# Plain tiles in program order, with the attention stages placed by hand between half products

## The chip, the cores and the metric

The kernel runs on one core of a Trainium2 chip. The metric is the device time of one execution in microseconds (us); of several executions the median is given. In the rows PE is TensorE's matmul engine and PEld its weight loads, DVE is VectorE, ACT is ScalarE, POOL is GpSimd, and SP is SyncE, on whose queue all of this kernel's DMAs are issued. L650 means line 650 of the kernel before.

## What is computed

Three layers on 4608 tokens of width 512 (8 batches of 576 tokens, 8 heads of 64). Inputs of the last two layers' weights are float64, all else is float32.

```python
k_p = k.reshape(B, H, Sp, 8, D).mean(axis=3)          # keys and values pooled by 8: 72 of each
v_p = v.reshape(B, H, Sp, 8, D).mean(axis=3)
scores = np.matmul(q, k_p.transpose(0, 1, 3, 2)) / np.sqrt(D)
attn = softmax(scores)                                 # with 1e-9 added to the sum
x = tokens(np.matmul(attn, v_p))                       # (4608, 512)
h = x @ w_in                                           # 512 -> 2048
x = np.maximum(0.01 * h, h) @ w_out                    # 2048 -> 512
xn = x / sqrt(mean(x * x) + 1e-6) * rms_g
out = (silu(xn @ w_gate) * (xn @ w_val)) @ w_out2      # 512 -> 1536 -> 512
```

## The kernel before

Every float32 product is made of three matmuls of rounded parts (`TERMS`: high by high, high by low, low by high), so a value that TensorE multiplies lies in SBUF as a pair of tiles HI and LO; `split` makes such a pair with a ScalarE copy and a VectorE (or GpSimd) subtraction.

The 4608 tokens are nine tiles of 512. Tiles 0 to 6 are the plain tiles (`PLAIN` is 7): their first feed-forward layer is done as plain products. Tiles 7 and 8 do the same layer later, as a pair, by Strassen's products, and after them five pairs do the last layer in the same way. What those need of sums and parts of weights is made during the plain tiles by side steps (`side_steps`), on ScalarE, VectorE and GpSimd, and stored to DRAM.

A plain tile `j` runs over sixteen blocks `f` of 128 hidden units. `h_unit` makes `h` for one block: 12 matmuls into a bank of PSUM (tag `h`, two banks), 512 columns each. ScalarE then applies the ReLU twice, once into the HI tile and once into the float32 tile `g` in SBUF, and VectorE subtracts the one from the other for LO (lines 646 to 650). `y_unit`, for the block two before, adds 12 matmuls into four banks that hold the tile's output; `y_store` copies these out at the end. In tile 0 eight blocks are done in two parts, of 256 columns each.

The tokens come from attention, which runs beside the plain tiles, 40 steps of 128 queries (a batch has five). For one such step `step_t` transposes the queries, `step_s` makes the scores in two halves and the softmax, `step_x` transposes the result; for a part of a batch (`av0` 256 tokens, `av1` 320) `step_av` makes the output for four pairs of heads. `k_prep` and `v_prep` pool keys and values (on GpSimd from batch 1 on), `step_kt` transposes the keys. All transposes, the scores and the outputs go through two banks of PSUM (tag `att`). `top_up` issues the loads of queries, keys and values as their buffers come free.

Batch 0's steps come before tile 0 or in its first part (`before`, `second`). The steps of the others (`seq`) are divided by `SHARE` over places: even places are plain tiles, in which the steps are dealt over the slots between `h_unit` and `y_unit` (`attention_slot`), odd places are borders, whose steps are all run one after another at the end of a tile (`for x in border[j]`, lines 1450 and 1451). Tokens of a plain tile that lie more than about one tile ahead are split, stored to DRAM (`x_early`, line 394) and loaded again when their tile comes (`x_tile_loads`, line 407), because only two buffers (tag `xhl`) hold tokens. The order of all this on each engine is not the program's: a planner, which estimates the length of each instruction, chooses it up to the end of the plain tiles. From line 1466 on (`begun`) each engine's instructions are chained in program order (lines 1597 to 1604); that is the last two blocks of tile 6 and all that follows.

The parts of `w_out` for tiles 2 to 6: eight blocks rest in SBUF, eight pass through a ring of four buffers (`next_wo`, `RING` 4, line 725); the buffers that this frees hold the side steps' tiles. In the pairs, `Quad.result` (line 1259) does the same ReLU as `h_unit`, with the subtraction on GpSimd.

Of the kernel before, what the change touches and what calls it, by code (L numbers as in the profile page):

```python
# [17 lines left out]

TG = 3
# [5 lines left out]
def pooled_attention_then_two_ffns(  # L25
# [14 lines left out]
    B, H, S, D = q.shape  # L40
    NT, DM = out.shape
# [12 lines left out]
    PLAIN = NJ - 2  # L54
    QT = [0, 128, 256, 384, S - P]
    EAGER = 1
    H_STEPS, G_STEPS, P_STEPS, SIDE_END = 2, 5, 4, 128
    SHARE = (0, 0.13, 0.3, 0.475, 0.65, 0.825)
# [32 lines left out]
    eps = per.tile([P, 1], F32, name="eps")  # L91
    gain = per.tile([P, KC], F32, name="gain")
    ones = per.tile([P, P], F32R, name="ones")
# [106 lines left out]
    nc.gpsimd.memset(eps, 1e-6)  # L200

# [21 lines left out]
    def load_q(b, t, tile_=None):  # L223
        x = ap.tile([P, 512], F32, tag="q", bufs=2, name=f"q{b}_{t}") if tile_ is None else tile_
        nc.sync.dma_start(
            out=x.rearrange("p (h d) -> p h d", h=H),
            in_=q[b, :, QT[t]:QT[t] + P, :].rearrange("h s d -> s h d"),
        )
        qraw[b, t] = x
# [24 lines left out]
    def v_prep(b, r):  # L254
# [17 lines left out]
        )  # L272
        if rest:
# [45 lines left out]
    def step_s(b, t):  # L319
# [7 lines left out]
        for half in range(2):  # L327
            pt = bank("att", 2, f"sc{b}_{t}_{half}")
# [12 lines left out]
            )  # L341
        nc.scalar.activation(out=e, in_=e, func=AF.Exp, scale=ESCALE)
        nc.vector.tensor_reduce(out=st[:, 1, :], in_=e, axis=AX.X, op=ALU.add)
        nc.vector.tensor_scalar(out=st[:, 1, :], in0=st[:, 1, :], scalar1=1e-9, scalar2=None, op0=ALU.add)
# [8 lines left out]
    def step_x(b, t):  # L353
# [14 lines left out]
        for g in range(2):  # L368
            (nc.scalar.copy if b < 2 else nc.vector.tensor_copy)(
                out=er[:, g].rearrange("p d (q k) -> p d q k", q=2),  # L370
                in_=e[:, 2 * g:2 * g + 2, P:].unsqueeze(1).to_broadcast([P, 3, 2, REST]),
            )
        pt = scratch(b, f"xt{b}_{t}")
# [3 lines left out]
        split(nc.scalar, a[:, :, HI, cols], nc.vector, a[:, :, LO, cols], src)  # L377
        pt = scratch(b, f"xr{b}_{t}")
# [10 lines left out]
    place = [-1]  # L389
    x_dram = {j: dram.tile([P, KC, N], F32, name=f"x{j}") for j in range(PLAIN, NJ)}  # L390
    xh_dram = {}
    x_loads = {}

    def x_early(j, p, a, z, src):

        if j not in xh_dram:
            xh_dram[j] = dram.tile([P, 2, KC, N], F32, name=f"xh{j}")
        while a < z:
            e = min(z, a + N // 2)
            t = per.tile([P, 2, N // 2], F32R, tag="tg", bufs=TG, name=f"xs{j}_{p}_{a}")[:, :, :e - a]  # L400
            split(nc.scalar, t[:, HI], nc.vector, t[:, LO], src[:, :e - a])
            nc.sync.dma_start(out=xh_dram[j][:, :, p, a:e], in_=t.bitcast(F32))
            if p == NP - 1:
                x_loads.setdefault(j, []).append((a, e))
            src, a = src[:, e - a:], e

    def x_tile_loads(j):
        todo = sorted(x_loads.pop(j, ()))
        while todo:
            a, z = todo.pop(0)  # L410
            while todo and todo[0][0] == z:
                z = todo.pop(0)[1]
            for h in range(2):
                nc.sync.dma_start(out=x_tile(j)[:, h, :, a:z].bitcast(F32), in_=xh_dram[j][:, h, :, a:z])

    def x_tile(j):
        if j not in xhl:
            xhl[j] = per.tile([P, 2, KC, N], F32R, tag="xhl", bufs=2, name=f"xhl{j}")
        return xhl[j]

    def step_av(b, ci, p):
# [15 lines left out]
        while t0 < b * S + c1:  # L437
# [3 lines left out]
            if j >= PLAIN:  # L441
                x = per.tile([P, N], F32, tag="tg", bufs=TG, name=f"xs{b}_{ci}_{p}_{j}")[:, :t1 - t0]
                nc.scalar.copy(out=x, in_=pt[:, o:o + t1 - t0])
                nc.sync.dma_start(out=x_dram[j][:, p, t0 - j * N:t1 - j * N], in_=x)
                t0 = t1
                continue
            if place[0] < 2 * j - 3:
                x_early(j, p, t0 - j * N, t1 - j * N, pt[:, o:o + t1 - t0])
# [3 lines left out]
            split(  # L452
                nc.scalar, x[:, HI, p, t0 - j * N:t1 - j * N],
                nc.vector, x[:, LO, p, t0 - j * N:t1 - j * N], pt[:, o:o + t1 - t0],
            )
# [70 lines left out]
    END = 2 * PLAIN - 3  # L526
    low, high = [], []
    for kind, b, t in seq:
        lo, hi = 0, END
        if kind.startswith("av"):  # L530
            t0, t1 = (b * S + c for c in CH[int(kind[2])][:2])
            lo = 0 if t1 <= N * 2 else 2 * max(0, min((t1 - 1) // N, PLAIN - 1) - EAGER) - 3
            hi = min(2 * (t0 // N) - 1, END)
        low.append(max([lo] + low[-1:]))
        high.append(hi)
    for i in reversed(range(len(seq) - 1)):
        high[i] = min(high[i], high[i + 1])
    places, now = [[] for _ in range(2 * PLAIN)], 0
    for i, x in enumerate(seq):
        assert low[i] <= high[i]  # L540
        here = 2 * sum(i >= c * len(seq) for c in SHARE[1:])
        here = min(max(here, low[i], now), high[i])
        if here % 2 and here > max(low[i], now):
            here -= 1
        elif here % 2 and here < high[i] and not x[0].startswith("av"):
            here += 1
        places[here].append(x)
        now = here
# [1086 lines left out]
```

## Time and profile before

| | us |
|---|---|
| median of 3 runs (1880.48 to 1887.28) | 1884.13 |
| the profiled execution, its own time | 1889.12 |
| its span, first to last instruction | 1887.4 |
| lead: attention of batch 0, first weights | 0 to 40 |
| tile 0, to the last store of its output | 40 to 204 |
| tiles 1 to 5 | 204 to 812 |
| tile 6, no attention | 812 to 904 |
| the pair of tiles 7 and 8, then the last layer's pairs | 904 to 1887 |

The ends of the stages are the times at which the last DMA of a tile's output (line 689) was issued. TensorE is the busiest engine, with 94% of the span; VectorE has 50%, ScalarE 37%, GpSimd 33%. The chain of work that ended last has 81% of its time on TensorE. So time is lost where TensorE stands still, or where its clock is granted at the lower of its two levels, 1.2 instead of 2.4 GHz: a stretch whose mean is given as 0.61 had the lower level most of the time.

### The profile page before, as it was taken

The page shows a single profiled execution, that of the slowest core. Times are in us where ns is not written, and L with a number is a line of the kernel's source. Part 1 is how long each engine was busy: PE and PEld are TensorE (multiplying, and loading weights), DVE is VectorE, ACT ScalarE, POOL GpSimd, SP SyncE. Part 2 cuts the span into 40 slices and gives each one's busy share as a digit, 9 for nine tenths or more (in the row PEclk, how much of TensorE's full clock was granted, in tenths as well). Part 3 has the DMA queues.
Part 4 walks back from the last instruction along what each step waited for, and adds up shares of the span by engine and source line. Part 5 has one row for each costly group of instructions (what it writes and reads, how often), then busy time and mean ns, then how long its engine had stood idle before and what let it go on. Part 6 is the DMA issues. An engine that isn't in the chain of part 4 may idle for free.

```text
span 1887.4 us, 24256 instructions
## 1 busy us (share of the span) xinstructions
PE 1782.9 (94%) x8548; PEld 1511.7 (80%) x8548; DVE 938.9 (50%) x1691; ACT 697.9 (37%) x1476; POOL 630.6 (33%) x761
## 2 busy tenths in 40 slices
PE   3797999989898899899999999999999999999999
PEld 3787887878687787788778888899888889988887
DVE  8865435465555455452476544524734443563331
ACT  5653333333444344342455333224323323332220
POOL 2445215453432422020455344134224403422330
PEclk7898999999898999899999999999999999999999
DMA  8954204545565565274999765677775568776552
GB/s 263 391 193 145 77 20 142 173 130 196 156 204 161 170 203 174 78 244 126 337 316 310 233 211 186 230 277 250 268 241 194 200 228 293 252 265 205 201 201 89
DMA packets 215241, 388.54 MB, mean 206 GB/s; under 512 B 60752, under 2 KB 122192, under 8 KB 214352
## 3 DMA queue, kind: packets, MB, share of 16 engines
q1 hardware_dynamic: 215120, 386.99, 61.3%
q8 instruction: 68, 1.11, 0.2%
q14 instruction: 53, 0.43, 0.1%
HBM read 306.71 MB, written 80.22 MB: 205 GB/s over the span
## 4 chain that ended last, share of the span: by engine, by line
PE 81%; DMA 6%; DVE 5%; ACT 3%; POOL 2%; issue 2%; SPq 1%; ACTq 0%; POOLq 0%; DVEq 0%
PE o L1382 15%; PE h L637 13%; PE y L673 13%; PE yg L1253 6%; PE yv L1253 6%; PE o L1362 4%; PE xg L1253 4%; PE xv L1253 4%; PE wg L1253 4%; PE wv L1253 4%; PE yh L1253 2%; PE sc L331 2%; DMA y<-ye 2%; PE wh L1253 1%; PE xh L1253 1%
## 5 line engine op out<-in xcount | busy, mean ns | idle before, releaser
L637 PE MATMUL h<-xhl,w_i 128*128 128x512 f32 (+1 forms) x1440 | 350.0, 390 | 6.4 <-ACT g L104 3.9
L1382 PE MATMUL o<-wo,u 128*128 128x512 f32 x1296 | 316.3, 392 | 4.1 <-DMA wo<-wo 4.0
L637 PEld LDWEIGHTS h<-xhl,w_i 128*128 128x128 f32 x1440 | 265.0, 196 | 58.9 <-ACT g L104 7.1
L1382 PEld LDWEIGHTS o<-wo,u 128*128 128x128 f32 x1296 | 243.4, 189 | 53.5 <-DMA wo<-wo 4.9
L673 PE MATMUL y<-ghl,w_o 128*128 128x512 f32 (+1 forms) x1104 | 239.3, 360 | 3.2 <-ACT ye L686 1.4
L673 PEld LDWEIGHTS y<-ghl,w_o 128*128 128x128 f32 x1104 | 183.6, 191 | 31.1 <-ACT ghl L104 1.9
L650 DVE TENSOR_TENSOR ghl<-g,ghl 128x512 fp32r<-128x512 f32 (+1 forms) x120 | 90.5, 755 | 169.3 <-ACT g L104 164.2
L101 POOL TENSOR_TENSOR u<-e2g,u 128x512 fp32r<-128x512 f32 (+1 forms) x25 | 29.7, 1189 | 311.2 <-ACT u L98 311.2
L104 ACT ACTIVATE ghl<-h 128x512 fp32r<-128x512 f32 (+1 forms) x120 | 68.1, 567 | 163.6 <-PE h L637 162.4
L673 PE MATMUL y<-ghl,wr 128*128 128x512 f32 x432 | 111.6, 396 | 1.1 <-ACT ghl L104 1.1
L673 PEld LDWEIGHTS y<-ghl,wr 128*128 128x128 f32 x432 | 79.2, 188 | 17.2 <-ACT ghl L104 1.5
L235 POOL TENSOR_TENSOR v<-v 128x256 f32<-128x256 f32 (+3 forms) x84 | 55.0, 660 | 89.5 <-DMA v<-in_v_dram 85.0
L1253 PE MATMUL yg<-T,ag 128*128 128x512 f32 (+1 forms) x360 | 84.0, 368 | 0.0
L1253 PE MATMUL yv<-T,av 128*128 128x512 f32 (+1 forms) x360 | 83.8, 368 | 0.0
L1253 PE MATMUL xg<-xa,ag 128*128 128x512 f32 (+1 forms) x360 | 83.8, 367 | 0.0
L1253 PE MATMUL xv<-xa,av 128*128 128x512 f32 (+1 forms) x360 | 83.7, 367 | 0.0
L1253 PEld LDWEIGHTS yg<-T,ag 128*128 128x128 f32 x360 | 66.0, 188 | 10.0 <-DVE e1v L1230 0.6
L1253 PEld LDWEIGHTS yv<-T,av 128*128 128x128 f32 x360 | 66.2, 188 | 9.5
L1253 PEld LDWEIGHTS xv<-xa,av 128*128 128x128 f32 x360 | 66.0, 188 | 9.6
L1253 PEld LDWEIGHTS xg<-xa,ag 128*128 128x128 f32 x360 | 66.1, 188 | 9.4
L104 ACT ACTIVATE g<-h 128x512 f32<-128x512 f32 (+1 forms) x120 | 68.0, 567 | 12.9 <-DMA xh<-xs 6.2
L427 PE MATMUL av<-at,vb 128*128 128x256 f32 (+1 forms) x192 | 45.8, 357 | 20.0 <-DVE xs L101 6.9
(213 smaller groups left out, 3155.5 us busy)
## 6 DMA issues: line engine op xcount, KB each, us to landing
wo<-wo SPq DMA_DIRECT2D x148, 512.0 KB
ag<-op_g SPq DMA_DIRECT2D x90, 512.0 KB
av<-op_v SPq DMA_DIRECT2D x90, 512.0 KB
wr<-wo SPq DMA_DIRECT2D x36, 512.0 KB
op_g<-parts_g SPq DMA_DIRECT2D x36, 256.0 KB
op_v<-parts_v SPq DMA_DIRECT2D x36, 256.0 KB
out_dram<-oe SPq DMA_DIRECT2D x36, 256.0 KB
q<-in_q_dram SPq DMA_DIRECT2D x35, 256.0 KB
```

The costliest lines, as they stand in the source:

```text
L101: lo_eng.tensor_tensor(out=lo, in0=src, in1=hi.bitcast(F32), op=ALU.subtract)
L104: return nc.scalar.activation(out=out, in_=in_, func=AF.Prelu, scale=scale, alpha=alpha)
L235: nc.gpsimd.tensor_tensor(out=x[:, :n], in0=x[:, :n], in1=x[:, n:2 * n], op=ALU.add)
L331: nc.tensor.matmul(pt[:, i * n:(i + 1) * n], y[:, p, :], kblk[b % 2][:, p * n:(p + 1) * n], start=True, stop=True,)
L427: nc.tensor.matmul(pt[:, :n], vb[b, p][:, sp].rearrange("p h d -> p (h d)"), a[:, p, mp, 0:n], start=i == 0, stop=False,)
L637: nc.tensor.matmul(pt, w[:, sp, c * P:(c + 1) * P], x[:, mp, c, :], start=c == 0 and i == 0, stop=c == n_k - 1 and i == 2,)
L650: nc.vector.tensor_tensor(out=t[:, LO, :], in0=g, in1=t[:, HI, :].bitcast(F32), op=ALU.subtract)
L673: nc.tensor.matmul(pt, w[:, sp, m * P:(m + 1) * P], g[:, mp, a - c0:a - c0 + n], start=ydone[j, a] == 1 and i == 0 and m % per_bank == 0, ...
L1253: nc.tensor.matmul(pt, wt[:, a, c, sp, :], xt[:, mp, :], start=start and c == 0 and i == 0, stop=c == 1 and i == 2, skip_group_check=not s ...
L1362: nc.tensor.matmul(pt, w[:, sp, m * P:(m + 1) * P], u[:, mp, :], start=f == blocks(q, z)[0] and i == 0, stop=f == blocks(q, z)[-1] and i == 2,
L1382: nc.tensor.matmul(pt, u[:, sp, m * P:(m + 1) * P], w[:, mp, :], start=f == 0 and i == 0, stop=f == F2 - 1 and i == 2,)
```

## The change

Tile 0's first 14 of 24 units of work (`TIED`) stay as they were: the planner orders them, and the steps of batch 1 up to its first output (`mine`) are dealt over units 8 to 13. From there on `begun` is set, so each engine follows the program's order. There is no border, and nothing is dealt by shares: the program counts points, one after each half of an `h` product (6 matmuls of 512 columns) and one after each half of a `y` product, 28 in the rest of tile 0, 64 in each of tiles 1 to 5 and 60 in tile 6. A step of attention is cut into stages (the functions become generators, with `yield` between stages), and `late_attention` names a point for each: scores at `s` and `s+1`, exponential at `s+3`, sum and division at `s+4`, copies at `s+6`, transposes at `s+7` and `s+8`, with `s` 7 points apart in tile 0, 11.25 and later 9 points apart afterwards. The side steps follow the same count (`SIDE_BEGIN` 84).

`x_early` and the stores and loads that go with it are gone. Instead tiles 3 and 6 have a third token buffer, in the places of blocks 4 to 7 of `w_out`; so blocks 0 to 11 of `w_out` now pass through the ring (`RING` 12, 12 loads a tile instead of 8). The ReLU's float32 value is written over `h` in PSUM, not into SBUF, and VectorE subtracts from there; in the pairs two of four such subtractions move from GpSimd to VectorE. The copies `er` are all on ScalarE. One side unit more falls to the pair of tiles 7 and 8.

```diff
+    H_STEPS, G_STEPS, P_STEPS, SIDE_BEGIN, SIDE_END = 4, 11, 9, 84, 356
-    H_STEPS, G_STEPS, P_STEPS, SIDE_END = 2, 5, 4, 128
-    SHARE = (0, 0.13, 0.3, 0.475, 0.65, 0.825)
     def x_tile(j):
         if j not in xhl:
-            xhl[j] = per.tile([P, 2, KC, N], F32R, tag="xhl", bufs=2, name=f"xhl{j}")
+            if j in (3, 6):
+                xhl[j] = [weight_slot(9 + 2 * c, f"xhl{j}_{c}") for c in range(KC)]
+            else:
+                t = per.tile([P, 2, KC, N], F32R, tag="xhl", bufs=2, name=f"xhl{j}")
+                xhl[j] = [t[:, :, c, :] for c in range(KC)]
+    def late_attention():
...
+        start = {7: 0, 8: 7, 9: 14}
+        for i in range(10, len(tiles) + 1):
+            start[i] = 22 + round(11.25 * (i - 10)) if i < 26 else 202 + 9 * (i - 26)
+        for i in range(FIRST_LATE, len(tiles)):
+            b, t = tiles[i]
+            s, after = start[i], start[i + 1]
+            stage(("s", b, t), (s, s + 1, s + 3, s + 4))
+            stage(("x", b, t), (s + 6, s + 7, s + 8))
+            if i + 1 < len(tiles):
+                stage(("t", *tiles[i + 1]), (s + 6,))
+            if t < 2:
+                for k in range(3):
+                    stage(("vp", b, 3 * t + k), (s + 2 * k, s + 2 * k + 2))
+            if t in (2, 3) and b + 1 < B:
+                for k in range(3 if t == 2 else 2):
+                    stage(("kp", b + 1, 3 * (t - 2) + k), (s + 4 * (t - 2) + 2 * k,))
+                stage(("kt", b + 1, t - 2), (after + 3,))
+            if t in (1, 4):
+                for p in range(NP):
+                    stage((f"av{t // 4}", b, p), (after + 2 + p,))
+    def h_parts(j, f, c0, pt):
...
         prelu(t[:, HI, :], pt, 0.01)
-        prelu(g, pt, 0.01)
-        nc.vector.tensor_tensor(out=t[:, LO, :], in0=g, in1=t[:, HI, :].bitcast(F32), op=ALU.subtract)
+        prelu(pt, pt, 0.01)
+        nc.vector.tensor_tensor(out=t[:, LO, :], in0=pt, in1=t[:, HI, :].bitcast(F32), op=ALU.subtract)
-    RING = 4
+    RING = 12
+    begun = len(nc.cur_bb.bb.instructions)
+    for i in range(TIED, len(jobs) + 2):
...
+        for i, x in enumerate(chunks):
+            x()
+            for f in at_spot.pop(i, ()):
+                f()
+            attention_point()
```

## Rows read from the trace of the kernel before

**Rows 1.** Busy time by stage: stretch, length, busy us (instructions), clock, DMA share, GB/s.

```profile
40.10:140.00 99.90, 87.98 (x568) 80.19 (x567) 75.20 (x149) 58.59 (x142) 44.22 (x61) 0.89 0.82 294
140.00:203.80 63.80, 53.25 (x347) 49.07 (x348) 34.77 (x76) 25.61 (x78) 33.04 (x65) 0.87 0.49 149
203.80:811.90 608.10, 565.14 (x2697) 468.19 (x2696) 310.49 (x682) 233.71 (x550) 195.19 (x303) 0.95 0.47 146
811.90:903.70 91.80, 90.14 (x396) 73.78 (x394) 35.63 (x57) 32.89 (x67) 17.54 (x18) 1.00 0.57 182
903.70:1030.00 126.30, 124.75 (x541) 102.53 (x541) 74.59 (x125) 63.98 (x131) 59.65 (x64) 0.99 0.96 328
```

The five busy columns are PE, PEld, DVE, ACT and POOL.

**Rows 2.** Groups by line, PE, tiles 1 to 5: count, busy us, mean ns.

```profile
L637 PE MATMUL h<-xhl,w_i 128*128 128x512 f32 x993 | 254.6, 403 | 2.6 <-ACT g L104 2.6
L673 PE MATMUL y<-ghl,w_o 128*128 128x512 f32 x624 | 161.3, 398 | 1.4 <-ACT ye L686 1.4
L673 PE MATMUL y<-ghl,wr 128*128 128x512 f32 x339 | 89.0, 397 | 1.1 <-ACT ghl L104 1.1
```

**Rows 3.** Timeline of PE inside tile 4: start, us, instruction and count, idle before.

```profile
628.15 2.89 PE L637 MATMUL h<-xhl,w_i 128*128 128x512 f32 x12
630.88 2.43 PE L673 MATMUL y<-ghl,w_o 128*128 128x512 f32 x10
633.15 0.60 PE L375 MATMUL xt<-ident,ex 128*128 128x128 f32 x4
633.59 0.38 PE L380 MATMUL xr<-ident,er 128*96 128x128 f32 x2
633.73 0.71 PE L673 MATMUL y<-ghl,w_o 128*128 128x512 f32 x2
```

**Rows 4.** Timeline of PE at a border, between tiles 3 and 4.

```profile
497.00 1.25 PE L331 MATMUL sc<-kblk,qT 128*128 128x144 f32 x8 [1.19 <-DVE at L101]
...
502.49 1.09 PE L375 MATMUL xt<-ident,ex 128*128 128x128 f32 x4 [2.06 <-DVE ex L346]
...
512.18 4.91 PE L637 MATMUL h<-xhl,w_i 128*128 128x512 f32 x12
```

**Rows 5.** Busy time of PE alone: three mixed stretches, two borders.

```profile
203.80:293.00 89.20, 89.20 (x442) 1.00 0.10 27
311.00:398.00 87.00, 81.86 (x389) 0.96 0.47 148
671.00:779.00 108.00, 104.40 (x517) 1.00 0.50 163
495.40:512.20 16.80, 9.59 (x39) 0.61 0.54 161
779.00:797.50 18.50, 10.82 (x47) 0.63 0.11 26
```

**Rows 6.** Groups by line, tiles 1 to 5, of POOL, DVE and ACT.

```profile
L785 POOL TENSOR_TENSOR hr<-w_i 128x256 f32<-128x256 f32 x32 | 26.1, 838 | 0.6
L798 POOL TENSOR_TENSOR hs<-hr,hs 128x512 fp32r<-128x512 f32 x16 | 20.6, 1288 | 28.9 <-ACT hs L794 28.9
...
L235 POOL TENSOR_TENSOR v<-v 128x256 f32<-128x256 f32 x18 | 14.3, 794 | 33.7 <-DMA v<-in_v_dram 33.7
...
L235 POOL TENSOR_TENSOR v<-v 128x128 f32<-128x128 f32 x18 | 10.1, 560 | 1.0
...
L269 POOL TENSOR_TENSOR vm<-vs,mask_main 128x128 f32<-128x128 f32 x19 | 8.9, 468 | 44.8 <-DVE vb L101 44.4
...
L265 POOL TENSOR_TENSOR vs<-v 128x64 f32<-128x64 f32 x18 | 7.8, 431 | 1.3
...
L650 DVE TENSOR_TENSOR ghl<-g,ghl 128x512 fp32r<-128x512 f32 x80 | 63.8, 797 | 114.1 <-ACT g L104 109.3 <-PE sc L331 4.5
...
L101 DVE TENSOR_TENSOR at<-xt,at 128x512 fp32r<-128x512 f32 x24 | 16.5, 687 | 31.7 <-ACT at L98 31.7
...
L98 ACT ACTIVATE at<-xt 128x512 fp32r<-128x512 f32 x24 | 14.4, 599 | 13.0 <-PE xt L375 13.0
```

More of the change, by code (lines that the diff above doesn't have):

```diff
@@ L525, in pooled_attention_then_two_ffns @@
     before, second = before[:at_], before[at_:]
[L526 to L548, printed above, removed]
-    by_tile, border = places[0::2], places[1::2]
+    FIRST_LATE = next(i for i, (b, t) in enumerate(tiles) if (b, t) == (1, 2))
+    cut = seq.index(("s", *tiles[FIRST_LATE]))
+    seq, late_seq = seq[:cut], seq[cut:]
+    mine = seq
+    assert mine[-1][:2] == ("av0", 1)
     def run_load(x):
@@ L578, in run_step, with put, stage, go @@
             top_up(1 if W1.left() else 3)
-        emit[kind](b, t)
+        for _ in emit[kind](b, t) or ():
+            pass
         if b > 0 and kind in use:
             live["q" if kind == "t" else "kv"] -= 1
+    at_point = {}
+    def late_attention():
+        def put(point, f):
+            at_point.setdefault(point, []).append(f)
+        def stage(key, points):
+            run = []
+            def go(first, last):
+                kind, b, t = key
+                if first:
+                    run.append(emit[kind](b, t))
+                if run[0] is not None:
+                    next(run[0], None)
+            for i, point in enumerate(points):
+                put(point, lambda i=i: go(i == 0, i + 1 == len(points)))
+            if key[0] in use:
+                def free():
+                    live["q" if key[0] == "t" else "kv"] -= 1
+                put(points[0] + 3, free)
+        start = {7: 0, 8: 7, 9: 14}
[18 more added lines that the diff above has]
+                    stage((f"av{t // 4}", b, p), (after + 2 + p,))
+    point_now = [0]
+    def attention_point():
+        for f in at_point.pop(point_now[0], ()):
+            f()
+        for f in side[point_now[0]] if point_now[0] < len(side) else ():
+            f()
+        point_now[0] += 1
+        if att is not None:
+            top_up(3)
     y_dram = [dram.tile([P, KC, N], F32, name=f"y{j}") for j in range(NJ)]
@@ L1366, in y_part @@
             if f == blocks(q, z)[-1]:
[L1367 removed]
+                t = e_tile(N, f"oe{q}_{z}_{m}")
                 if m % 2:
@@ new lines, in attention_slot, with convert @@
+    def attention_slot():
+        for x in plan.pop(0) if plan else ():
+            run_step(x)
+    def convert():
+        if W1.left():
+            W1.step()
+    late_attention()
+    late_end = max(at_point) + 1
+    for i, (f, c0, c1) in enumerate(jobs[:TIED]):
+        h_unit(0, f, c0, c1)
+        attention_slot()
+        if i >= 2:
+            y_unit(0, *jobs[i - 2])
+        for _ in range(3 if f > 10 else 2):
+            convert()
+        attention_slot()
+    assert not plan
@@ L1399, in pooled_attention_then_two_ffns @@
+    assert not W1.left()
+    y_store(0)
+    for j in range(1, PLAIN):
+        at_spot = {}
         last = j == PLAIN - 1
         if last:
[L1401 removed]
+            assert point_now[0] >= late_end
             begin_phase2()
[L1403 to L1411 removed]
@@ L1447, in pooled_attention_then_two_ffns, with put @@
-        while plan:
-            attention_slot()
-        place[0] += 1
-        for x in border[j]:
-            run_step(x)
-        if last:
-            assert not early and not side
-            break
-        y_unit(j, *jobs[-2])
-        y_unit(j, *jobs[-1])
-        y_store(j)
-    pieces = [lambda x=x, ms=ms: y_unit(PLAIN - 1, *x, ms) for x in jobs[-2:] for ms in ((0, 1), (2, 3))]
-    pieces.append(lambda: y_store(PLAIN - 1))
+        def put(i, x):
+            at_spot.setdefault(i, []).append(x)
@@ L1595, in pooled_attention_then_two_ffns @@
         assert not early + late
+    assert point_now[0] >= len(side) and not at_point
     before_on = {}
```

265 lines of the change are left out of this document (131 added, 134 removed).

## The prediction

> **What bounds the kernel now.** I read the stages first [rows 1]. In every stage but the first two TensorE is busy for about 93% or more of the time, so the question is not which engine is the bound but how much of TensorE's time is neither plain work nor attention. The reader should see three kinds of stage there: tile 6, which has side steps but no attention, is busy for 90.1 of 91.8 us at full clock; tiles 1 to 5 are busy for 565.1 of 608.1 us, at a granted clock of 0.95; the rest of tile 0 (140 to 203.8) for 53.3 of 63.8 us, at 0.87. The loss sits where attention runs.
>
> How much it is follows from a count. Tiles 1 to 5 hold 993 + 624 + 339 = 1956 plain matmuls [rows 2]. Twelve of them undisturbed take 630.88 - 628.15 = 2.73 us, 0.2275 us each [rows 3]: 445.0 us. The other 2697 - 1956 = 741 matmuls [rows 1] are attention's; four transposes take 633.59 - 633.15 = 0.44 us, 0.11 us each [rows 3]: 81.5 us. Together 526.5 us of work in 608.1 us, so **81.6 us are lost**. Of these 43.0 us are plainly idle, and a clock of 0.95 takes about 0.05 x 608 = 30 us; the rest is gaps that modelled ends cover.
>
> Then I looked for the place. Inside a tile attention costs little beyond its work: the transposes stand between two products with no wait [rows 3], a mixed stretch of 89.2 us has no idle time at all, and one of 108 us has 3.6 us, both at full clock [rows 5]. At the borders it is another picture: from 497.0 to 512.2 no plain matmul runs; transposes wait for the softmax, scores for the split before them [rows 4]. That border is 16.8 us long with 39 matmuls, 4.3 us of work, at a clock of 0.61; the one at 779 is 18.5 us long with 47, 5.2 us of work, at 0.63 [rows 5]. Each loses 12 to 13 us, and idle time lowers the clock of what runs in it and just after it. So most of the loss is chains of dependent attention steps with nothing between them.
>
> **The change, part by part.** *Tiles 1 to 5.* The borders go. Each stage now follows half a product (6 x 0.2275 = 1.36 us), and stages that depend on each other through ScalarE or VectorE are mostly two or three points, 2.7 to 4.1 us, apart. The longest chain between two points is sum, division and product of the softmax; its users come two points (copies) and three points (transposes) after it. What remains I take as a share of the 526.5 us of work. Tile 6, in which attention can disturb nothing, loses 1.8% [rows 1]; mixed stretches of the old order lose 0%, 3.3% and, the worst, 5.9% idle with a clock of 0.96 [rows 5]. I take 4%, 21 us, because the old mixed stretches had the same work and no fixed distances, and the new ones share two banks at successive points: **81.6 - 21 = 60 us gained**. Bounds: 1.8% leaves 9.5 us (72 gained), 6% leaves 32 us (50 gained).
>
> *The rest of tile 0* (28 points). Now 10.5 us idle and 0.13 x 63.8 = 8.3 us of clock, 19 us [rows 1]. The three steps of batch 1 are placed 7 points apart. The last output of `av1` comes at point 27, and the first half product of tile 1 that reads it is the second one, so about 1 us of wait stays there; with 4% of 44 us, 3 us remain: **16 us gained** (12 to 18).
>
> *Tile 0's first units and the lead* keep planner and order. Their 11.9 us of idle and 11 us of clock [rows 1] stay. There are now 24 steps of batch 1 over 12 slots, where 33 were dealt over 23; I take 0, from 5 gained (fewer steps before the end) to 5 lost (they are denser, and one load of keys or values at a time is allowed there).
>
> *Tile 6 and the pairs.* One more side unit in the pair: a raw load of 512 KB and stores of 768 KB, 1.3 MB, in a stage whose DMA engines are 96% busy at 328 GB/s [rows 1]: 4 us of transfer if all of it showed. TensorE was still busy for 124.8 of 126.3 us there, so most is hidden: **2 us lost** (0 to 6).
>
> *The ReLU in PSUM.* ScalarE writing PSUM is not in the trace. The nearest row, 512 columns read from PSUM and written to SBUF, is 0.60 us [rows 6]. At nothing gained or at double, 0.6 us x 16 a tile, about 10 us more of an engine that is busy for 234 of 608 us, it stays beside TensorE's work: I take 0.60 us and no effect. VectorE's subtraction took 0.80 us from SBUF; with one operand in PSUM a subtraction of the same size takes 0.69 us [rows 6], so VectorE is if anything relieved, by 0.11 us x 16 a tile. The bank of `h` is held until then, some 2 to 3 us after the product's end; its next product begins 7 points later, 9.5 us. Cover gone, it would cost that difference per block.
>
> *The moved DMAs.* Four more loads of `w_out` a tile, 2 MB, stand against the removed stores and loads of tokens; the DMA engines are 47% busy [rows 1]. A load is issued 14 points, 19 us, ahead of its use. All DMAs now pass SP's queue in program order: a load that waits for its buffer holds later ones back, but keys and values are three buffers ahead and stores wait two points. I take 0; if a `w_out` load came late, the `y` product would wait for it directly. `er` on ScalarE adds about 0.5 us a step there and takes as much from VectorE: 0.
>
> *Sum*, against the profiled execution's 1889.1 us: 1889.1 - 60 - 16 + 2 = 1815 us. The median of the runs is 1884.1 us, 5 us under it, and carries over: **1810 us**, 3.9% less. The case's own ends: 1884 - 72 - 18 - 5 = 1789 and 1884 - 50 - 12 + 5 + 6 = 1833.
>
> **The rivals.** *1. Two banks at successive points.* After the second and fifth step of a batch, scores, outputs, queries and transposes use the two `att` banks at nine points in a row. A bank must be free two points later, about 3.2 us with attention's own matmuls. Copy and subtraction take 0.60 + 0.69 us [rows 6] on empty queues; behind one ReLU (0.60) and one subtraction (0.80) 2.7 us. The margin is 0.5 us, so a third instruction ahead makes TensorE wait. There are 33 x 5 + 52 + 12 = 229 groups of attention matmuls from point 0 on (two scores and three sets of transposes a step, 52 outputs, 12 for keys). At 0.15 us on the average that is 34 us: **1844 us**. For it: the waits at a border for exactly this [rows 4]. Against: in mixed stretches they did not show [rows 3, 5].
>
> *2. The clock.* If the short waits that remain are spread so that the clock stays at a mean of 0.95 all along, 5% of 526 us, 26 us, stay: **1836 us**. Against it: the clock is 1.00 in two of three mixed stretches, and low at the borders [rows 5]. The Trainium skill has such a case ("TensorE: Matmul & The Clock Gate", section "A second HAM failure mode: psum-queue depth-cycling"): cycling through PSUM banks can make short idle times between groups frequent enough for the clock to swing between its levels. By that rule the spread order would do worse than I forecast; the mixed stretches at 1.00 speak against it here.
>
> *3. Slower: ScalarE and VectorE held at the head of their queues by GpSimd.* In points 84 to 148 a side unit takes GpSimd 2 x 0.84 + 1.29 = 2.97 us every four points, and a value block 0.79 + 0.56 + 0.43 + 0.47 = 2.25 us every two points while a run of three lasts [rows 6]. Four points are about 6.1 us: 49% and 74%, more than GpSimd has. It falls some 2 us behind, and in program order the split of the values and the sums of the side unit then stand ahead of the scores' evacuation; nobody may pass. There are 66 blocks of keys and values and 16 such units, 82 meetings. From 74/82 = 0.9 us of TensorE each the gain is gone; at 1.5 us it is 123 us: 1810 + 123 = **1933 us**. Against it: only the 16 units overload GpSimd, which is busy for 195 of 608 us now [rows 1], and the stages are two points apart.
>
> *4. No change*: rival 1 at twice its price, 0.33 us a group, 75 us: about **1884 us**.
>
> **How the numbers follow.** Forecast 0.66, rival 1 0.17, rival 2 0.04, rival 4 0.04, rival 3 0.09. A measurement of this kernel can tell about 0.3%, 6 us, from no change. Faster by more: 0.66 + 0.17 + 0.04 = 0.87; within it 0.04; slower 0.09. The range takes the forecast's ends, 1789 to 1833, with 2 us below for a gain of the pair's stage, and reaches over rivals 2 and 1 with some room: 1787 to 1850.
>
> **What would show it.** Right: no stretch of 10 us in tiles 1 to 5 without a plain matmul; a granted clock of 0.98 or more from tile 1 on; a plain tile with attention in some 110 us where it was 122; the wait of transposes for the softmax product gone from TensorE's waits. Rival 1 shows as waits of scores and outputs for `at`, `xhl` and `xs` splits, rival 3 as waits of ScalarE and VectorE for `vm` and `hr`, rival 2 as a clock under 0.97 without long gaps. The prediction is wrong if tiles 1 to 5 lose more than 6% of their time, or if tile 0's planned part grows by more than 10 us.

## The result, and the profile after

| | before | after |
|---|---|---|
| median, us | 1883.87 (1880.48 to 1887.28) | 1809.67 (1808.22 to 1811.55) |
| ratio, 95% interval | | 0.9607 [0.9586, 0.9627] |
| span of the profiled execution, us | 1887.4 | 1809.1 |
| mean granted clock | 0.967 | 0.985 |
| lead | 40.1 | 40.8 |
| tile 0 | 163.7 | 156.1 |
| tiles 1 to 6 | 699.9 | 630.0 |
| pairs | 983.7 | 982.2 |

The change makes the kernel 3.9% faster. The differences of the four stages, +0.7, -7.6, -69.9 and -1.5, add up to the span's -78.3 us, and nearly all of it comes from tiles 1 to 6. Tiles 1 to 5 are not compared by length alone, because the ends of stages are DMA issues and a few matmuls lie on the other side of them now.

Busy time by stage of the kernel after: stretch, length, busy us of PE, PEld, DVE, ACT and POOL (instructions), clock, DMA share, GB/s. The stages are the planned part of tile 0, its rest, tiles 1 to 5, tile 6 and the pairs.

```profile
40.80:140.00 99.20, 81.75 (x508) 73.13 (x507) 75.91 (x152) 59.70 (x144) 49.80 (x66) 0.86 0.49 154
140.00:196.90 56.90, 55.19 (x421) 52.93 (x422) 30.48 (x71) 25.27 (x76) 15.69 (x31) 1.00 0.19 56
196.90:728.30 531.40, 527.76 (x2639) 441.23 (x2638) 283.45 (x617) 237.24 (x591) 196.43 (x330) 1.00 0.61 196
728.30:826.90 98.60, 98.60 (x437) 81.64 (x436) 35.06 (x54) 35.50 (x71) 14.17 (x17) 1.00 0.56 188
826.90:1809.10 982.20, 972.84 (x4503) 829.21 (x4501) 455.19 (x682) 328.92 (x595) 328.00 (x288) 1.00 0.69 241
```

Against [rows 1]: in tiles 1 to 5 TensorE now stands still for 3.6 us, where it was 43.0, and the clock is 1.00 where it was 0.95. ScalarE and GpSimd have as much to do there as before, VectorE 283 us instead of 310. The first row is the exception, with a clock of 0.86 and 17.5 idle us.

All that TensorE waited for in tiles 1 to 5 of the kernel after: who waited for whom, us in total, times, longest.

```profile
PE xt L380 <- DVE xhl L99: 2.0, 1, 2.0
PE av L412 <- DVE ex L340: 0.8, 1, 0.8
PE xt L380 <- DVE ex L350: 0.7, 1, 0.7
```

The same of the kernel before, its first four rows:

```profile
PE xt L375 <- DVE ex L346: 11.1, 5, 5.2
PE av L427 <- DVE xs L101: 6.9, 5, 2.5
PE qt L309 <- issue: 5.2, 3, 3.1
PE sc L331 <- DVE xs L101: 4.0, 3, 1.6
```

Three of these rows are waits of a chain in which each stage needs the one just before it: transposes for the softmax product (`ex`), outputs and scores for the evacuation of the bank they write; `issue` names no engine. Of such waits three are left, 3.5 us in all.

The timeline of PE in the kernel after, in tile 4 (start, us, instruction and count, idle before), shows what stands in their place:

```profile
592.11 0.66 PE L333 MATMUL sc<-kblk,qT 128*128 128x144 f32 x4
592.50 1.64 PE L702 MATMUL y<-ghl,wr 128*128 128x512 f32 x6
593.98 0.65 PE L333 MATMUL sc<-kblk,qT 128*128 128x144 f32 x4
594.38 1.65 PE L702 MATMUL y<-ghl,wr 128*128 128x512 f32 x6
```

Each piece of attention lies between two half products. Compare [rows 4], where pieces of the same kind follow each other for 15 us. Over tiles 1 to 5 the longest time between two plain matmuls is now 2.8 us (380.03 to 382.80).

### The profile page after: what moved, and what is told of

Same layout as the page of the kernel before. It is cut to its first block, busy times and chain, and to the rows that moved or that the text cites. A ratio compares the mean times of both kernels' runs of the same rounds, so it can differ in the third digit from the quotient of the medians.

```text
span 1809.1 us, 24150 instructions
## 1 busy us (share of the span) xinstructions
PE 1748.5 (97%) x8548; PEld 1487.6 (82%) x8548; DVE 911.1 (50%) x1629; ACT 707.2 (39%) x1528; POOL 613.5 (34%) x756
## 4 chain that ended last, share of the span: by engine, by line
PE 88%; DVE 5%; DMA 3%; ACT 1%; issue 1%; POOL 1%; SPq 1%; POOLq 0%; ACTq 0%; DVEq 0%
PE o L1424 15%; PE h L661 15%; PE y L702 15%; PE yg L1296 6%; PE yv L1296 6%; PE o L1404 4%; PE xg L1296 4%; PE xv L1296 4%; PE wg L1296 4%; PE wv L1296 4%; PE sc L333 2%; PE yh L1296 1%; PE av L412 1%; PE wh L1296 1%; PE xh L1296 1%
## 5 line engine op out<-in xcount | busy, mean ns | idle before, releaser
L661 PEld LDWEIGHTS h<-xhl,w_i 128*128 128x128 f32 x1440 | 254.3, 192 | 45.3 <-DVE ghl L679 2.9
L679 DVE TENSOR_TENSOR ghl<-h,ghl 128x512 fp32r<-128x512 f32 (+1 forms) x120 | 78.5, 654 | 209.1 <-ACT h L102 208.9
L702 PE MATMUL y<-ghl,w_o 128*128 128x512 f32 (+1 forms) x864 | 175.1, 349 | 0.0
L702 PE MATMUL y<-ghl,wr 128*128 128x512 f32 x672 | 172.4, 399 | 0.0
L702 PEld LDWEIGHTS y<-ghl,w_o 128*128 128x128 f32 x864 | 136.5, 191 | 16.8
L702 PEld LDWEIGHTS y<-ghl,wr 128*128 128x128 f32 x672 | 123.5, 189 | 23.2
L1296 PE MATMUL xv<-xa,av 128*128 128x512 f32 (+1 forms) x360 | 83.7, 367 | 0.0
L102 ACT ACTIVATE h<-h 128x512 f32<-128x512 f32 (+1 forms) x120 | 67.9, 566 | 0.0
L96 ACT ACTIVATE u<-e2g 128x512 fp32r<-128x512 f32 (+1 forms) x30 | 17.7, 590 | 120.6 <-DVE e2g L1327 120.6
L1273 DVE TENSOR_TENSOR e6g<-yg,e1g 128x512 f32<-128x512 f32 (+1 forms) x30 | 19.2, 638 | 81.8 <-PE yg L1296 72.4
```

Source lines behind the costliest of these rows:

```text
L96: nc.scalar.activation(out=hi, in_=src, func=AF.Copy)
L102: return nc.scalar.activation(out=out, in_=in_, func=AF.Prelu, scale=scale, alpha=alpha)
L661: nc.tensor.matmul(pt, w[:, sp, c * P:(c + 1) * P], x[c][:, mp, c0:c1], start=c == 0 and i == 0, stop=c == KC - 1 and i == 2,)
L679: nc.vector.tensor_tensor(out=t[:, LO, :], in0=pt, in1=t[:, HI, :].bitcast(F32), op=ALU.subtract)
L702: nc.tensor.matmul(pt, w[:, sp, m * P:(m + 1) * P], g[:, mp, a - c0:a - c0 + n], start=ydone[j, a] == 1 and i == 0 and m % per_bank == 0, ...
L1273: nc.vector.tensor_tensor(out=out, in0=u, in1=w, op=ALU.add)
```

## The experiments

The theory: a fixed order with several half products between stages that depend on each other through ScalarE or VectorE removes both the idle time and the low clock after it. A point is the place behind one half product, 6 matmuls. The rivals: the fixed order alone does it; the new program does it under any order; the traffic that was removed does it; the ReLU in PSUM does it. None of the kernels leaves out a part of the computation; `e7_more_traffic` adds stores that nobody reads. No run takes apart what the copies `er` on ScalarE or the moved subtractions of the pairs do alone.

### The new program, ordered by the planner through tile 6

The point from which the order is fixed moves from unit 14 of tile 0 to the end of tile 6.

```diff
-    begun = len(nc.cur_bb.bb.instructions)
     for i in range(TIED, len(jobs) + 2):
...
+    begun = len(nc.cur_bb.bb.instructions)
     def queue_out(q, z, fs):
```

> The changed kernel with its points, third token buffer and ReLU as they are, but the chain that fixes program order begins only after tile 6, so the planner orders tiles 0 to 6 again. Theory (the gain is the distance between dependent attention stages, filled with plain work): the distances stand in the program, but the planner may put plain work ahead of them or pull stages together; 1810 to 1840 us if it keeps them apart, more if it does not. Rival (the fixed order of each engine is itself the gain, whatever the distances): 1850 us or more, with stretches of attention without a plain matmul as before.

Measured: 1858.26 us (1855.24 to 1859.49), 0.9863 [0.9848, 0.9878] of before. Two thirds of the gain, 1858 - 1810 = 49 of 74 us, are gone with the fixed order; the planner keeps 25. Its tiles 1 to 5, by the columns of the stage table:

```profile
178.30:793.50 615.20, 575.56 (x2766) 0.96 0.46 149
```

By the prediction's count this stage holds 2005 plain matmuls and 761 of attention, 456.1 + 83.7 = 539.8 us of work: 75 us are lost, where it was 82 before and is 17 in the change. So in tiles 1 to 5 the new places bring little under the planner; most of the 25 us that it keeps lie in tile 0, which takes 136.3 instead of 163.7 us with 36 matmuls fewer.

The planner runs attention in a row again, as in [rows 4]: from 639.5 to 661.1 us and from 764.2 to 791.2 us no plain matmul runs. PE in this kernel, inside tiles 1 to 5:

```profile
645.82 0.96 PE L309 MATMUL qt<-ident,q 128*128 128x128 f32 x4 [1.86 <-issue]
649.02 1.09 PE L380 MATMUL xt<-ident,ex 128*128 128x128 f32 x4 [2.25 <-DVE ex L350]
...
651.52 2.29 PE L333 MATMUL sc<-kblk,qT 128*128 128x144 f32 x8 [0.99 <-DVE at L99]
```

So the stages' places in the program are of little use if the order on the engines is chosen anew.

### The old program, chained in program order from tile 1 on

```diff
+    begun = None
     for j in range(PLAIN):
+        if j == 1:
+            begun = len(nc.cur_bb.bb.instructions)
...
-    begun = len(nc.cur_bb.bb.instructions)
```

> The kernel before, its steps dealt whole over the slots as they were, but each engine chained in program order from tile 1 on; nothing else of the change. Theory: the program of before has no distances (scores and softmax are one piece, the transposes follow one to three slots later), so order alone exposes the chains and loses more than the planner did: 1900 to 1990 us. Rival (order itself is the gain): 1810 to 1850 us.

Measured: 1934.61 us (1932.08 to 1944.98), 1.0287 [1.0254, 1.032]: 51 us slower than before. What PE waited for in its tiles 1 to 5 (first two rows):

```profile
PE xr L380 <- DVE er L369: 47.1, 16, 7.3
PE qt L309 <- issue: 11.2, 6, 1.9
```

The fixed order by itself is a loss for this program. It writes the stages of a step one after another, and in program order TensorE stands at `xr` until VectorE has made `er`. The time came as expected, by another wait than the expected chain: the transposes wait only 6.8 us for the softmax product, where it was 11.1 before. What holds `er` is other work ahead of it in VectorE's queue. In the longest of these waits it is a value's split (`vb`), and that waits through ScalarE for GpSimd:

```profile
465.93 0.42 ACT L276 ACTIVATE vb<-vm 96x256 fp32r<-96x256 f32 x1 [2.94 <-POOL vm L269]
466.38 0.42 DVE L278 TENSOR_TENSOR vb<-vm,vb 32x256 fp32r<-32x256 f32 x1 [2.66 <-ACT vb L276]
467.23 0.63 PE L380 MATMUL xr<-ident,er 128*96 128x128 f32 x2 [7.31 <-DVE er L369]
```

The change also has all copies `er` on ScalarE, and the old program with that alone was not run; how much of the 51 us it would take away stays open. Neither half of the change, as it was tested, does it alone: new places under the planner 1858, old places in a fixed order 1935, both together 1810 us.

### The distance between the stages, taken away and halved

No distance: scores, softmax and transposes of a step follow each other, with the same fixed order.

```diff
-            stage(("s", b, t), (s, s + 1, s + 3, s + 4))
-            stage(("x", b, t), (s + 6, s + 7, s + 8))
+            stage(("s", b, t), (s + 5, s + 6, s + 6, s + 6))
+            stage(("x", b, t), (s + 6, s + 6, s + 8))
```

> The changed kernel with the second half of the scores, exponential, sum and division, copies and first transposes of a step all at one point (s+6) instead of s+1, s+3, s+4, s+6 and s+7: no plain work between dependent stages of the softmax, all else equal. Theory: each of the 33 steps shows TensorE the whole chain, 5.2 us as in the wait of 5.19 us before the transposes at 789.7 in the kernel before, 172 us, and 1 to 2 us more each where the clock falls to its lower level: 1980 to 2050 us. Rivals (program order, less DMA traffic, the ReLU in PSUM): within 10 us of 1810 us, since none of them is touched.

Measured: 2022.29 us (2015.81 to 2023.19), 1.0729 [1.0709, 1.0748]. Half the distance:

```diff
-            stage(("s", b, t), (s, s + 1, s + 3, s + 4))
+            stage(("s", b, t), (s + 3, s + 4, s + 5, s + 5))
```

> The changed kernel with scores at s+3 and s+4, exponential and sum at s+5, the transposes at s+7 as they are: three points instead of six between the last scores and the transposes. Theory: three points are 4.1 us of plain work and 0.5 to 1 us of other attention, the chain is 5.2 us and up to 1 us of queues; 0.1 to 1.6 us shown per step, 33 steps: 1813 to 1860 us. Rivals: within 10 us of 1810 us.

Measured: 1835.54 us (1831.59 to 1839.89), 0.9745 [0.9726, 0.9764]: 26 us over the change, clear of the noise. The transposes' wait for the softmax product in tiles 1 to 5, in the kernel with no distance and then in the one with half of it; in the change it is 0.7 us, once:

```profile
PE xt L380 <- DVE ex L350: 130.6, 30, 6.0
```

```profile
PE xt L380 <- DVE ex L350: 18.7, 18, 2.5
```

From the second half of the scores to the transposes there are six points in the change, three with half the distance and none without: 1810, 1836 and 2022 us, with one wait, eighteen and thirty. One of the thirty in the kernel with no distance, PE's timeline:

```profile
612.38 0.65 PE L333 MATMUL sc<-kblk,qT 128*128 128x144 f32 x4
617.55 1.09 PE L380 MATMUL xt<-ident,ex 128*128 128x128 f32 x4 [4.51 <-DVE ex L350]
618.43 1.06 PE L309 MATMUL qt<-ident,q 128*128 128x128 f32 x4
619.14 2.91 PE L661 MATMUL h<-xhl,w_i 128*128 128x512 f32 x6
```

The wait is 4.5 us, and the six matmuls of `h` behind it take 2.91 us where others take 1.64: from 617.5 to 622.1 us the granted clock is 0.50, the lower of its two levels, so the wait is paid for a second time. That is in the stage as well (length 725.6 us against 531.4, clock 0.89 against 1.00). The second row is the same stage with half the distance, where the waits are shorter and the clock stays at 0.99:

```profile
212.20:937.80 725.60, 596.22 (x2663) 0.89 0.44 143
200.80:756.30 555.50, 534.25 (x2636) 0.99 0.57 187
```

### The traffic that was removed

Sixteen more stores of 512 KB in each of tiles 1 to 4, 33.5 MB in all.

```diff
+        if j < 5:
+            for f in range(F1):
+                put(4 * f + 1, lambda f=f: nc.sync.dma_start(out=junk[f], in_=W1.done["i", f].bitcast(F32)))
```

> The changed kernel with 16 more stores of 512 KB in each of tiles 1 to 4 (parts of w_in to DRAM that nobody reads), 33.5 MB in all: over three times the 10 MB of token stores and loads that the change removed, on the same queue and DMA engines. Theory (the removed traffic is no part of the gain, as TensorE waited for none of it): 1805 to 1815 us. Rival (the removed round trip through DRAM carries half of the 74 us): its price would be 3.7 us a MB, 33.5 MB would cost 50 us or more.

Measured: 1810.73 us (1810.14 to 1811.25), 0.9619 [0.96, 0.9638], as the change itself. In tiles 1 to 5 the DMA engines move 259 instead of 196 GB/s, and the length is the same within 2 us:

```profile
196.10:726.00 529.90, 526.36 (x2640) 440.44 (x2639) 282.68 (x618) 237.60 (x592) 197.27 (x331) 1.00 0.75 259
```

The removed stores and loads of tokens brought nothing by being fewer.

### The ReLU in PSUM: undone in the change, and alone in the kernel before

```diff
-        prelu(pt, pt, 0.01)
-        nc.vector.tensor_tensor(out=t[:, LO, :], in0=pt, in1=t[:, HI, :].bitcast(F32), op=ALU.subtract)
+        g = per.tile([P, N], F32, tag="tg", bufs=3, name=f"g{j}_{f}_{c0}")[:, :n]
+        prelu(g, pt, 0.01)
+        nc.vector.tensor_tensor(out=t[:, LO, :], in0=g, in1=t[:, HI, :].bitcast(F32), op=ALU.subtract)
```

> The changed kernel with the ReLU's float32 value of the plain tiles written to SBUF again, as before, and subtracted from there. Theory: ScalarE and VectorE have time to spare beside TensorE, so nothing moves: 1805 to 1815 us, though VectorE's subtraction goes from 0.65 back to about 0.75 us, 11 us more of VectorE in all. Rival (the value in PSUM carries part of the gain, by VectorE's shorter queue): 10 us or more slower than 1810 us.

Measured: 1816.62 us (1814.61 to 1817.94), 0.965 [0.963, 0.9669]: 7 us over the change, so the edit is not free of effect. The opposite edit in the kernel before:

> The kernel before with only the ReLU's float32 value of the plain tiles kept in PSUM. Theory: VectorE is busy half the time and not the bound, the stalls are chains of attention: 1878 to 1888 us. Rival (part of the gain): 10 to 30 us faster than 1883 us.

Measured: 1871.16 us (1868.8 to 1872.22), 0.9938 [0.9922, 0.9954]: 11 us less. But its tiles move both ways: tile 0 takes 152.3 us where it took 163.7, tile 4 takes 143.1 where it took 128.8. There the planner makes another order, and the 11 us can't be put down to the ReLU. In the fixed order the 7 us can. The subtraction in tiles 1 to 5, first with the value in PSUM (after), then in SBUF: count, busy, mean ns, idle before.

```profile
L679 DVE TENSOR_TENSOR ghl<-h,ghl 128x512 fp32r<-128x512 f32 x79 | 54.6, 691 | 133.6 <-ACT h L102 133.6
```

```profile
L680 DVE TENSOR_TENSOR ghl<-g,ghl 128x512 fp32r<-128x512 f32 x80 | 64.0, 800 | 133.7 <-ACT g L102 127.5 <-PE av L417 6.2
```

The mean is 0.11 us shorter, as forecast from [rows 6], but the mean hides two kinds. Shortest, median and longest in ns, first in PSUM, then in SBUF:

```profile
L679 DVE TENSOR_TENSOR ghl<-h,ghl x79: 677/692/695, 198.8 to 720.7; 128x512 fp32r<-128x512 f32 x79
L680 DVE TENSOR_TENSOR ghl<-g,ghl x80: 680/693/2593, 198.3 to 726.0; 128x512 fp32r<-128x512 f32 x80
```

With the value in SBUF, the 45 subtractions beside which GpSimd did nothing, or for less than 0.05 us, took 0.69 us each; the other 35, which overlap in time with work of GpSimd, took 0.94 us on the average and 2.59 at most. With the value in PSUM all 79 took 0.69 us or a little less, 33 of them beside GpSimd. So VectorE is later just where GpSimd works. The largest single place is tile 2, 111.3 instead of 107.5 us, where a wait of TensorE for a bank (`av` for `ex`) is 1.9 us instead of 0.8.

### The one queue that stands: a side unit's sums, one point later

The 2.0-us wait in tile 2 of the change, by engine (start, us, idle before):

```profile
378.66 2.25 DVE L802 TENSOR_TENSOR hr<-hr 128x128 f32<-128x128 f32 x4
378.88 0.40 POOL L268 TENSOR_TENSOR vm<-vs,mask_main 128x128 f32<-128x128 f32 x1 [1.54 <-DVE vb L99]
379.24 1.51 POOL L823 TENSOR_TENSOR hr<-w_i 128x256 f32<-128x256 f32 x2
380.83 0.21 DVE L99 TENSOR_TENSOR xhl<-av,xhl 128x64 fp32r<-128x64 f32 x1
381.07 0.38 ACT L96 ACTIVATE xhl<-av 128x256 fp32r<-128x256 f32 x1 [3.99 <-DVE xhl L99]
382.06 1.09 PE L380 MATMUL xt<-ident,ex 128*128 128x128 f32 x4 [2.03 <-DVE xhl L99]
```

Read from below: TensorE needs a bank that VectorE has not emptied; VectorE comes late to the split `xhl` because the sums `hr` of a side unit stand ahead of it in its queue; these need parts that GpSimd makes until 380.75. GpSimd is itself late behind a block of values, for which it had stood 1.5 us until VectorE had done an earlier split (`vb`): each of the two queues holds the other. ScalarE stands for 4.0 us as well. The test gives GpSimd one point more:

```diff
-            for i, f in zip((0, 2, 4, 5, 8), (rebuilt, four, high, low, store)):
+            for i, f in zip((0, 3, 5, 6, 9), (rebuilt, four, high, low, store)):
```

> The changed kernel with the side units' four sums (VectorE) and the steps after them one point later, so that VectorE meets GpSimd's sum when it is done. In the changed kernel VectorE stood 2.25 us at these sums at 378.7 us, ScalarE 4.0 us behind it, and TensorE 2.0 us for the bank. Theory (a queue's head held by GpSimd reaches TensorE there, and nowhere else in tiles 1 to 5): that wait goes and the lower clock after it, 2 to 4 us, 1806 to 1809 us. Rival (other work ahead in VectorE's queue does it): no change, 1809 to 1812 us.

Measured: 1806.44 us (1805.36 to 1808.85), 0.9596 [0.9576, 0.9615]. Tile 2 takes 102.7 us instead of 107.5. Two waits of TensorE in it are changed: the one of 2.0 us is 0.3 now, and the one of 0.8 us, at 315.9 us, is gone. Together they had cost almost 5 us with the clock after the longer one (0.98 in that tile, 1.00 now); from 382.0 to 385.6 us it was 0.53, and six `y` matmuls took 2.84 us where others take 1.64. The whole gains about 3 us, by the ratios 2, and the two intervals overlap, so the gain as a whole is not shown; it is the fastest version of this study. With this edit and the value in SBUF together:

> As the run before, with the ReLU's float32 value in SBUF again, which alone cost 7 us (1816.6). If those 7 us come through the same wait (tile 2 took 111.3 instead of 107.5 us there), they go with it: 1808 to 1812 us. If VectorE's longer subtraction costs TensorE something by itself, spread over the tiles: 1813 to 1817 us.

Measured: 1810.21 us (1809.54 to 1811.34), 0.9614 [0.9596, 0.9633], 3.8 over the one above. So about half of the 7 us goes through the sums of the side units in tile 2. The rest is in tile 0 (157.5 against 154.7 us) and in tile 2 (104.7 against 102.7). In tile 0 the `y` product now waits 4.2 us in three times for the subtraction, a wait that the run above doesn't have; further it was not taken apart.

### The planned part of tile 0

By the work done in it, it came out some 6 us worse than before (worked out below). The longest of its waits, 4.4 of 17.5 idle us, is TensorE's for a copy of ScalarE, and ScalarE's for a part of the weights:

```profile
91.61 0.70 ACT L102 ACTIVATE raw_o<-raw_o 128x512 f32<-128x512 f32 x1 [4.74 <-DMA raw_o<-in_moe_w_out_dram]
93.81 0.45 ACT L373 COPY er<-ex 128x96 f32<-128x96 f32 x2
94.14 0.66 PE L386 MATMUL xr<-ident,er 128*96 128x128 f32 x2 [4.41 <-ACT er L373]
```

Two causes were tried. The 24 steps of batch 1 dealt more thinly, over 16 slots instead of 12, which leaves the rest of batch 0 11 slots instead of 15:

```diff
-    for n, items in ((2 * HALVES - 1, second), (2 * (TIED - HALVES), mine)):
+    for n, items in ((2 * HALVES - 5, second), (2 * (TIED - HALVES) + 4, mine)):
```

> The changed kernel with batch 0's remaining steps dealt over 11 instead of 15 slots and batch 1's first 24 steps over 16 instead of 12, all in the planned part of tile 0. It asks what made that part some 6 us worse than before the change. If it is the denser dealing of batch 1's steps: 3 to 6 us faster, 1803 to 1807 us. If it is ScalarE held by a weight part that has not landed (4.7 us at 91.6 us in the changed kernel), the dealing changes little or makes it worse: 1808 to 1815 us.

Measured: 1810.99 us (1810.48 to 1815.39), 0.9629 [0.9609, 0.965]; tile 0 takes 156.6 us, 156.1 without the edit. This dealing is no better; as it thins one part and thickens the other, the density of batch 1's steps is not tested alone. Then the fixed order from tile 1 on only, so that the planner has all of tile 0:

```diff
-    begun = len(nc.cur_bb.bb.instructions)
     for i in range(TIED, len(jobs) + 2):
...
     y_store(0)
+    begun = len(nc.cur_bb.bb.instructions)
```

> The changed kernel with all of tile 0 left to the planner, points and stages as they are, and the program order from tile 1 on. In the changed kernel the planned part of tile 0 stands still at 84 to 98 us, and the planner may not fill it, as the plain work after unit 13 is chained behind. In the run with the planner throughout, tile 0 held 113 us of work in 136 us where the changed kernel holds 120 in 156. Theory (it is the chain's early start that costs tile 0): 8 to 12 us faster, 1797 to 1802 us. Rival (batch 0's chain of steps sets tile 0 whatever the order): 1807 to 1812 us.

Measured: 1812.13 us (1810.84 to 1812.87), 0.9623 [0.9605, 0.9642]. Tile 0 is shorter, 150.8 us, but tile 1 is longer, 111.5 us: 39 matmuls only moved past the border. The wait of `xr` for ScalarE's `er` is still there, 4.9 us before 92.75.

Both edits of this and the section before together:

> The changed kernel with the program order from tile 1 on and the side units' sums one point later: the two edits of runs e9 and e11 together. They touch different tiles, so their gains should add: 1794 to 1800 us if both hold, 1807 to 1812 us if neither does.

Measured: 1807.98 us (1805.32 to 1809.69), 0.9598 [0.9579, 0.9617]; at most the sums' part holds. Under the planner all the way (the first experiment) tile 0 takes 136.3 us (42.0 to 178.3), 20 us less than in the change. Some 8 us of that are 49 matmuls that stand in later tiles; why it fills tile 0 better by the other 12 stays open.

## Why the prediction was right

**The mechanism, and the time of tiles 1 to 5: right.** It was said that the loss is chains of dependent steps with nothing between them, and that distance under plain work takes them away. The distances 6, 3 and 0 show it, with 1810, 1836 and 2022 us. Distance is not enough by itself: under the planner the same places lose 75 us in tiles 1 to 5. Of what was to be seen: no time over 2.8 us without a plain matmul (10 were named), a clock of 0.98 or more in each of the tiles, and plain tiles of 101.4 to 110.2 us where some 110 were named. One line of each tile's PE, with clock, DMA share and GB/s at the end:

```profile
196.90:299.90 103.00, 103.00 (x515) 1.00 0.40 136
299.90:407.40 107.50, 104.67 (x515) 0.98 0.84 277
407.40:516.70 109.30, 109.30 (x558) 1.00 0.58 181
516.70:626.90 110.20, 109.47 (x560) 1.00 0.62 194
626.90:728.30 101.40, 101.32 (x500) 1.00 0.59 187
```

**Its size.** By the prediction's own count, tiles 1 to 5 of the change hold 944 + 528 + 432 = 1904 plain matmuls and 2639 - 1904 = 735 of attention:

```profile
L661 PE MATMUL h<-xhl,w_i 128*128 128x512 f32 x944 | 244.6, 400 | 0.0
L702 PE MATMUL y<-ghl,wr 128*128 128x512 f32 x528 | 137.8, 401 | 0.0
L702 PE MATMUL y<-ghl,w_o 128*128 128x512 f32 x432 | 110.6, 399 | 0.0
```

At 0.2275 and 0.11 us that is 433.2 + 80.9 = 514.1 us of 531.4: 17.3 us lost, 3.4%, where 4%, 21 us, were taken. The gain of the term is 81.6 - 17.3 = 64 us, not 60. Tile 6 no longer loses its 1.8% either (98.6 busy of 98.6 us).

**Where the chains stood: wrong.** The prediction speaks of borders and says that the borders go. The windows of PE of the kernel before, tile 3 and tile 5 by their last output's DMA:

```profile
430.60:550.10 119.50, 111.79 (x528) 0.93 0.57 177
...
678.90:811.90 133.00, 121.72 (x587) 0.95 0.46 147
```

The stretch at 495 us lies inside tile 3, the one at 779 inside tile 5. And the numbers of steps in the fourteen places, worked out from `SHARE`, are 44, 0, 36, 0, 40, 0, 44, 0, 44, 0, 44, 0, 0 and 0: every border's list is empty. The stretch in [rows 4] stands between the `h` products of two blocks of tile 3; there the planner had left attention in a row, as it does again in the first experiment. The readings of time were right, and the cause that was named for the place was not: it is the planner's order, not the border loop. The times of [rows 4] and the ends of the tiles, side by side, would have shown it. Nor do the two stretches of [rows 5] carry the step from "each loses 12 to 13 us" to "most of the loss": they make 25 of 81.6 us. The kernel before has four more stretches of over 5 us without a plain matmul (11.9, 7.7, 7.0 and 5.5 us), all inside tiles.

**Rest of tile 0: right.** Idle time fell from 10.5 to 1.7 us and the clock rose from 0.87 to 1.00. By the prediction's own count, idle time and clock, 18.8 us lost became 1.7: 17 us gained, where 16 were forecast. The stage itself is only 6.9 us shorter, since it took over work from the planned part, 421 matmuls where it had 347.

**Planned part of tile 0: wrong, outside its bounds.** Forecast 0, within 5 either way. By the same count it lost 17.5 + 0.14 x 99.2 = 31.3 us, where [rows 1] give 11.9 + 11.0 = 22.9: 8 us worse. By work it is some 6 us: at 142 us, 192 `y` matmuls of 256 columns had run where it was 244, and 52 of them at 0.12 us are missing. What was missed: the moved DMAs were costed by queue order in tiles 1 to 5 only. In tile 0 the loads of weights share SP's queue with loads of keys and values, and ScalarE waits 4.7 us for one. That wait is seen; that it is the cause is not shown, for neither of the two edits cured it. It does not look like a lack of DMA bandwidth: the stretch moves 154 GB/s where it moved 294, since stores of weights went to later tiles, and in the 8 us of this wait (84 to 92) it is 191.

**ReLU in PSUM: wrong.** Forecast no effect, measured 7 us. The prices were right as means (594 and 691 ns, against 0.60 and 0.69 us), and two things were not. The 0.80 us from SBUF were read as the price of every subtraction, where one takes 0.69 us alone and more only beside GpSimd's work. And it was taken that VectorE has time to spare: it has on the average, 283 of 531 us, but not at the points where its queue stands behind GpSimd.

**Pairs and traffic.** The pairs came out 1.5 us shorter where 2 us longer were forecast; the additional 1.3 MB don't show, and what made the pairs shorter was not taken apart. That DMA traffic plays no part was right, and shown by 33.5 MB more.

**The rivals.** Rival 1, two banks at successive points, would have taken 34 us; all waits of TensorE in tiles 1 to 5 make 3.5 us, and the two of this kind, for a bank not yet emptied, 2.8. Rival 2, a clock of 0.95 all along, did not come: 1.00 in four tiles of five and 0.98 in the one with the 2.0-us wait. Of the rule that was set beside it, in the Trainium skill ("TensorE: Matmul & The Clock Gate", section "A second HAM failure mode: psum-queue depth-cycling"), nothing is seen here, though the two banks are cycled through all along: TensorE stands still for only 3.6 us in 531. With half the distance it stands still for 21 us, and the clock is still 0.99. Rival 3, VectorE and ScalarE held by GpSimd, reached TensorE in tile 2 alone, where 82 meetings were counted for it: the two waits there that went with the later sums cost almost 5 us with the clock, and about half of what the value in SBUF costs goes the same way. It does not change the sign. Rival 4, twice the price of rival 1, falls with it.

**The sum.** Against the profiled execution, 1889.1 us became 1810.8: -78.3, where -60 - 16 + 2 = -74 was forecast. The carry of 5 us from the profiled execution to the median was wrong in its turn: after, it is 1810.82 - 1809.67 = 1.2 us. The median's change, -74, agrees with the forecast because these two errors of 4 us cancel, as do the terms of tile 0's parts against each other. The 1810 is in part luck; that tiles 1 to 5 would give between 50 and 72 us is what the working earned.

## What to carry to other kernels

Find the chains that run uncovered by counting work against time for each stage, then look at what stands between two dependent steps. Here six half products between the scores and the transposes hid the chain, and three left eighteen short waits. It held only with the order on the engines fixed, and fixing the order of the old program was a loss. Where a program is ordered by a planner, look up which code stands behind a stretch of the trace before you name it as the cause. An engine with half its time to spare can still be late at one point: look for an instruction at the head of its queue that waits for a slower engine.

## What the runs showed of the hardware

- ScalarE writes 512 columns over their own place in PSUM in 594 ns; from PSUM to SBUF the same kernel takes 597. The Trainium skill ("ScalarE: Activation LUTs", section "Step-by-step: what each stage is for") calls PSUM the faster destination; at this size the trace shows no difference.

```profile
L102 ACT ACTIVATE ghl<-h 128x512 fp32r<-128x512 f32 x79 | 47.2, 597 | 130.8 <-PE h L661 128.4 <-issue 2.1
L102 ACT ACTIVATE h<-h 128x512 f32<-128x512 f32 x79 | 46.9, 594 | 0.0
```

- A float32 subtraction of 512 columns on VectorE with both operands in SBUF took 0.69 us where GpSimd did nothing beside it (45 of 80), and 0.94 us on the average, up to 2.59, where GpSimd worked at the same time (35 of 80). With one operand in PSUM it took 0.69 us or a little less all 79 times, 33 of them beside GpSimd. The two programs differ in one edit.
- A short wait of TensorE can be paid for again at the lower clock: behind one of 2.0 us the granted clock was 0.53 for 3.6 us, and behind one of 4.5 us it was 0.50 for 4.6 us, with six matmuls in 2.84 and 2.91 instead of 1.64 us. Not every wait is: eighteen of 18.7 us in all, 2.5 at most, left the mean clock of tiles 1 to 5 at 0.99.
- 33.5 MB of additional stores, at 259 instead of 196 GB/s, cost nothing that can be told from the noise beside a busy TensorE (1810.7 against 1809.7 us).
